# A fused LSH attention and FFN kernel: the probabilities of two head pairs of the first 256 tokens go through fp16 halves and DMA turns instead of fp32 turns on TensorE

## The chip, the cores and the metric

The kernel runs on one core of one Trainium2 chip. The metric is the device time of one execution in microseconds, the median of several runs; lower is better. The kernel before took 817.67 us (median of 3 runs, 816.54 to 818.07).

Five engines work in parallel, each through its own instructions in order: PE (TensorE, matrix products; its weight loads are listed as PEld), DVE (VectorE), ACT (ScalarE), POOL (GpSimd) and SP (SyncE, which here issues all DMA transfers). An instruction waits on semaphores for those of other engines on which it depends, and everything behind it on its engine waits too.

## The reference

```python
q_bits = (np.einsum('bhsd,dk->bhsk', q, proj) > 0)      # 6 hash bits per token, the same for k
mask = q_bucket[:, :, :, None] == k_bucket[:, :, None, :]
scores = np.where(mask, scale * (q @ k.T), -1e9)
attn = exp(scores - max); attn = attn / (attn.sum(-1) + 1e-9)
x = attn @ v                                            # 4 batches, 8 heads, 768 tokens, 64 dims
h = x.reshape(3072, 512) @ w_in                         # 512 -> 2048
g = h * np.tanh(softplus(h))                            # mish
out = g @ w_out                                         # 2048 -> 512
```

The inputs are 64-bit floats in memory and are converted on the chip. The products need more than fp16's precision. Most of the kernel gets it from two fp16 halves of each factor (a high half, and a low half that holds the rest) and three products: high by high, low by high, high by low. In the first units, fp32 products are used in some places, since those need no splitting ahead of them.

## The kernel before

**Units and slots.** The 3072 tokens are 12 units of 256 tokens (three per batch). A unit's attention is 8 slots: 4 pairs of heads by 2 blocks of 128 queries. Slot n of unit 0 has pair n // 2. One slot runs through this chain:

- S (`att_front`): PE multiplies the 128 queries with 768 keys of both heads into PSUM. The scores of slots 0 to 7 go alternately to `ps_s` and `ps_b`, later ones all to `ps_s`.
- Row maximum (DVE, L978), then scale and bias (`mb`, on DVE at L961 to L968 or on POOL at L972 and L973).
- Two exponentials (`att_exp`, ACT, L991), one per head, into a ring of three fp32 tiles `pb`, with the row sums.
- `att_back`: the sums' reciprocals (L1021), then the probabilities are turned (keys onto partitions) into `PT`, a ring of two pairs.
- V (`att_pv`): PE multiplies values with turned probabilities; the result goes to `X`, the unit's token block for the FFN.

**The two ways to turn.** In unit 0 (`if u == 0`), `pe_turn` turns the fp32 tile on PE: groups of three 128x128 turns (L434) into the PSUM tile `ps_l`, every fourth into `ps_t`, each group followed by a copy on ACT (L437) or DVE (L438). A group must wait until the bank's last copy is done. The probabilities are not yet divided by their sums: PE spreads the reciprocals over a tile (`rb`, L1072), ACT or DVE copies it (`rc`, L1075, L1076), V is an fp32 product (L1062) and DVE multiplies (L1079). In all other units the tile is first split into halves (`hl`): the high half is probability times reciprocal in fp16 (L390 on POOL, L392 on ACT, L393 on DVE), the low half the rest (L408 on DVE, one instruction; on POOL two, L414 and L415). One DMA turn per head and slot (L472) brings both halves to `PT`, and V is an fp16 product of three parts (L1088, two pairs at a time).

**Keys and queries.** In unit 0, pairs 0 and 1 have fp32 scores (L948): the keys are turned (L450) and their hash words come from a product with the sign weights `pw` (L461; `pw` is filled by DVE at L530). Pairs 2 and 3 have fp16 keys in two halves, turned by DMA, with hash bits (L739, L743, L748), and scores at L937.

**FFN.** For each unit 8 steps H (`ffn_h`, first product), mish on ACT, then O (`ffn_out`, second product). In unit 0 they are fp32 (L1120, L1169), later fp16 halves (L1130 to L1132, L1179 to L1181). H0, the first of all, needs all four pairs of unit 0 in `X`. The weights come in as 64-bit floats, are joined to fp32 (L594, L597, L601, L607), and are split later (`w_split`).

**What sets the order.** All operations are recorded with their alternatives (engine and cost), and `ORDER` is a table of numbers that gives the order in which they are issued, with a letter for the alternative (a, or none, is the first). The table fixes each engine's order and which engine does what; nothing is decided at run time. Semaphores are set from the dependences.

Of the kernel before, what the change touches and what calls it, by code (L numbers as in the profile page):

```python
# [23 lines left out]
PT = 12  # L24
# [69 lines left out]
137 7 9 8 50 20 0 5 11 19 12 22 1 2 3 4 76 80 29 81b 13 37 6 77b 14 15 10 25 33 26 30b 38 17 27 28 18 34 39 52  # L94
60 61 35 62 41 56 54 63 57 55 21 42 48 51 53 24 23 31 78 36 32 64 65 16 86 91 138 92 79 87 147 40 88 82 117 83
43 118 44 119b 93 89 66 109 110 111 153 90 94 120 67 112 154b 132 107d 46 108 133 113 95 115 68 114 116 124
125b 155 121 126 101 84 45 134 136 135 156 127b 178 96 128 140b 148 141 47 58 149 85 122d 123 97 99 142 139b
98b 143 129 168d 179 180d 100 174 176 69 175 177 170 130 157 171b 131 172 173b 204 205b 169 70 145b 182 189
144b 102 158 159 181 161b 190b 71 193 291 194 195 185 191 150 186 192 220 221 103 222d 183b 187 206 160b 196
188 197 104 223 212 152 146 49 151 162 59 105 106 213b 207 216 218 217b 219b 214 215b 184 353 224 243 163 239  # L100
164 244 245b 241 248 240 242 233c 270 368 307 210d 208 235 254 236 255 249 209b 237 246 238 247 225 256 271
250 257 234 272d 262 263 268 266 292 198 273 226 267b 211 227 293 165 294 269 251 283 284 349 350 264 303 265
285 295 166 304b 354 305 296 258 199 200 309d 286b 310 311c 260c 261 306 274 281 313 253 252 232 228 282 312b
322 201 317 364 287 365 288 289 290 366 318 319 355b 323 324 308 320 321 367 330b 331 315 338 339 72 231 203
202 167 229 397 369b 314 329 316 325 297 298b 275 276b 340 333 341 230 332b 334 342 73 370d 299 336 425c 277
74 426 371 399 378 379 380 335 328 302 400 398 300 373 424 423 351 337 301 280 381 427 372b 374 382 389c 411
376 259 375 278 279 406 429 458 428 390 412 452 407 352 391 383 384b 393 392c 395 326 327 385 453 408d 409 410
415d 343 344c 356c 416 451 430 456 345 431 432 394 377 459 386 418 346 457 396 401 417b 454 433 387 348 347
413 419 455 75 357 434 443d 488b 460 421 444 461 420 388 422 441 404 435 436 414 402 445 489 490b 447 437 462d
463 464 478d 403 446c 449 479 405 465 438 466b 471 472b 487 523 518 493 494 495c 486 358 359 467 496 480b 482b  # L110
497 448 481b 484 360 491 510 525 532 511 442 450 361 512b 533 534 535 362 526 524 468 483 513b 492 439 546 514
474 536 552 485 469 470 537 519b 475c 476 516 473 520 538c 539 553 515 517 586 540b 521 554 440 477 498 499b
500 501 555d 542 522 541c 556 557 573b 574 575 548 549b 550 527 503 502 544 577 590 545 543 578 528 530 504
505b 591 592 547 588 506 594 593 507 576b 595d 587 581 612 603 604 551 582 583b 579 596 598c 529 559 558 531
589 597 613 599 580 363 618 600 560 561 562 614d 616 584b 615 632c 563 564c 601 566 651 508 509 585 633 647
634c 648 655 659 640 617 567 649 636 650 652 664 653 605 635 656 565 619 620 621 660 654 638 622 623c 625 568
569 602 639 661d 609 668 606 641 663 662 681b 682 683c 642 626 637 570b 691 607b 608 685 657 665 666 571b 627
692 628 693d 572 624b 643b 782 672 644 645c 646 695 694 669 610b 658 723c 724 629 630b 684b 687 696 734 735
670b 673 783 697 675 725b 727 736d 738 686 726 631 698 737 688 690 689 732 786 731 749 674 667 699c 701 729
740d 741 791 742c 744 676 728 787 788 700 750 751 702 730 745 799 703 704 706 743b 677b 671 678 746 739 733  # L120
803 781 752 753 773b 800 784c 774 776 775 785 790 679b 804 705b 707 708 710 709 711 794 748 824 712 801c 779
777b 795 796c 802b 789 713 792 714c 716 780 747 778 825 839 680 798 797 816c 817 818b 715b 819 826 827 828 829
820 822 830 807 808 842 611 717 754 755 821 847 823 810 831b 832 833b 809 811 756 757 805 843 844 845 835 846
840 718 859 841 836 834c 719 721b 720b 758 759 860 722 760 837 838 769 861 871 872 863 873b 874 812 862b 864
875 876d 806 813 762 866 793 877 887 891 888 761 889b 892 865 879b 895 763 867 896 897d 898 848 878c 882 890b
880 868 884 904 764 765 885b 893c 899 883 881 849 850c 900 770 923 766b 852b 913b 914 771 767 922 908 924 768
925 905 901 915 916 926 917 927 928c 853 772 909 918 894 919 1026 920 929 930c 906 939 932b 910 902b 911 912
940 814b 869 968 854 921 972 941d 943 942 954 851c 903 931c 934 907 855 857 945 946 856 955 956c 947b 949b 969
973 1027 957 958 959c 937 936 982 970c 1028 933 935 960 961 948b 951b 858 971 963 976 815 944 977 978 979c 950
964 952 962 965b 938 986 967 953 981 980 995c 974c 1029 1067 1031 983 987 1005 1004 996 997c 999b 975b 988  # L130
998b 1001b 1006 1007b 1009 1008 966 1066 1010 1011 1012b 990 1158 1021 870 886 1032 1192 1193 984b 993 991 992
994 1022 1023 1019 1003 1033 1069 1030 1194 1024 1000 1014 1025 1039d 1050 1002 1015 1223 1068 985 1013c 1040
1016b 1017 1051 1052d 1041c 1070 1071c 1053 1043 1054 1195 1055c 1042b 1034 1044 1073 1018 1082 1077 1020 1038
# [20 lines left out]
1465c 1467 1408 1496 1512d 1383 1807 1516 1513 1514 1528d 1455 1456 1497 1529 1474 1385 1386 1519 1538 1520
1539 1540c 1499 1587 1517b 1530b 1532b 1541 1387 1468 1469 1483 1498 1542 1543c 1544 1545 1484 1470 1531b
1518b 1534 1591 1466c 1427c 1521 1522 1554 1641 1277 1500 1642 1523 1588 1547b 1555 1643 1556 1533 1535 1537
1536 1583 1508b 1557 1558 1509 1428 1584 1524 1569 1471b 1546b 1472b 1548 1473 1429c 1560b 1561 1570 1571c
# [1188 lines left out]
```

## Time and profile before

| | before |
|---|---|
| median of 3 runs | 817.67 us |
| the profiled execution's own time | 817.2 us |
| its span, first to last instruction | 815.4 us |
| granted TensorE clock | 1.0 |
| busy share PE, DVE, ACT, POOL | 98, 74, 77, 52% |
| starts on PE: S0, S4, S6, S8, S9, S10, H0 | 14.9, 37.0, 46.4, 56.0, 64.4, 71.6, 73.9 us |
| starts of V0, V1, V2, V3 | 40.7, 51.6, 61.7, 68.9 us |
| HBM read, written | 35.65, 6.29 MB |

The page gives each engine's busy time and its share of the span. A view by stage gives the same in chosen stretches; the timeline lists instructions of one engine in order of time, with the idle time ahead of each and what ended it; the groups put together instructions of one line and shape, with their mean duration; the waits add up who waited for whom. An engine's line shows how long an instruction takes, and the difference between two starts what it costs in a dense row, which on PE is less, since products overlap.

### The profile page before, as it was taken

Reading aid. Unit: us, or ns where it says so; the run is one execution under the profiler, and the core shown is the slowest. Engines: PE = TensorE matmul, PEld = TensorE weight load, DVE = VectorE, ACT = ScalarE, POOL = GpSimd, SP = SyncE. Lnnn points to the kernel's source line nnn. Section 1 sums busy time; section 2 is a strip of 40 time slices with the busy share of each in tenths; the row PEclk is TensorE's granted clock in tenths of the full one; section 3 lists DMA queues with packets and bytes.
Section 4 is the critical chain, followed back from the end, with each engine's and each line's share of the span. In section 5 each row is a group of like instructions: output and inputs, shape, how many; then the busy total and the mean of one; then the engine's idle time right before and its main releaser. Section 6 shows DMA issues by size and latency. Waiting matters only on the chain.

```text
span 815.4 us, 17000 instructions
## 1 busy us (share of the span) xinstructions
PE 798.2 (98%) x6546; PEld 549.6 (67%) x6546; DVE 602.9 (74%) x1103; ACT 624.9 (77%) x976; POOL 426.9 (52%) x434
## 2 busy tenths in 40 slices
PE   8899999999999999999999999999999999999998
PEld 5556666666676776676666676667676676776674
DVE  5888999988898778887887767768877675566211
ACT  4889998888696769889679698989779785677211
POOL 3564446554356773733585564344646758845120
PEclk9999999999999999999999999999999999999999
DMA  7958998989999969989989959999989577466200
GB/s 253 219 174 221 240 246 196 191 156 206 217 160 182 203 116 181 170 158 216 185 172 155 195 117 151 197 213 192 167 140 169 107 139 145 81 124 133 50 27 27
DMA packets 395489, 134.29 MB, mean 165 GB/s; under 512 B 365456, under 2 KB 386448, under 8 KB 395408
## 3 DMA queue, kind: packets, MB, share of 16 engines
q1 hardware_dynamic: 395408, 133.21, 81.2%
q8 instruction: 51, 0.84, 0.4%
q14 instruction: 30, 0.25, 0.1%
HBM read 35.65 MB, written 6.29 MB: 51 GB/s over the span
## 4 chain that ended last, share of the span: by engine, by line
PE 47%; ACT 1%; DVE 1%; DMA 1%; issue 0%; POOL 0%; SPq 0%; ACTq 0%; DVEq 0%
PE ps_s L937 7%; PE ps_o L1179 6%; PE ps_o L1181 6%; PE ps_o L1180 6%; PE ps_acc L1130 5%; PE ps_t L1088 5%; PE ps_acc L1132 5%; PE ps_acc L1131 5%; ACT pb L991 1%; DVE svb L978 1%; DMA out_dram<-ffb 1%; PE ps_t L739 0%; ACT L1315 0%; DVE hl L408 0%; ACT tok L480 0%
## 5 line engine op out<-in xcount | busy, mean ns | idle before, releaser
L991 ACT ACTIVATE pb<-ps_s,svb 128x768 f32<-128x768 f32 x184 | 180.9, 987 | 87.4 <-DVE svb L968 36.7
L978 DVE TENSOR_REDUCE svb<-ps_s 128x2 f32<-128x1536 f32 x92 | 161.3, 1753 | 40.2 <-PE ps_s L937 33.7
L1130 PE MATMUL ps_acc<-X,wo 128*128 128x256 f16 x616 | 167.9, 273 | 0.3 <-ACT ffb L1151 0.3
L1132 PE MATMUL ps_acc<-X,wo 128*128 128x256 f16 x616 | 167.9, 273 | 0.0
L1131 PE MATMUL ps_acc<-X,wo 128*128 128x256 f16 x616 | 167.9, 273 | 0.0
L1315 ACT ACT_TABLE_LOAD x117 | 150.1, 1283 | 2.0
L408 DVE SCALAR_TENSOR_TENSOR hl<-pb,svb,hl 128x768 f16<-128x768 f32 x131 | 140.3, 1078 | 13.8 <-POOL hl L390 9.8
L1181 PE MATMUL ps_o<-wi,ffb 128*128 128x512 f16 x352 | 133.4, 379 | 0.0
L1180 PE MATMUL ps_o<-wi,ffb 128*128 128x512 f16 x352 | 133.4, 379 | 0.0
L1179 PE MATMUL ps_o<-wi,ffb 128*128 128x512 f16 x352 | 133.4, 379 | 0.0
L937 PE MATMUL ps_s<-KT,QT 128*128 128x512 f16 (+1 forms) x656 | 120.1, 326 | 2.1 <-ACT pb L991 1.8
L390 POOL TENSOR_SCALAR hl<-pb,svb 128x768 f16<-128x768 f32 x68 | 71.0, 1046 | 75.9 <-DVE svb L1021 28.8
L937 PEld LDWEIGHTS <-QT 128*128 128x128 f16 x672 | 64.2, 98 | 40.5 <-issue 8.3
L1088 PE MATMUL ps_t<-PT,VT 128*64 128x256 f16 x1584 | 90.7, 273 | 0.0
L1088 PEld LDWEIGHTS <-VT 128*64 128x64 f16 x1584 | 84.8, 110 | 8.1 <-issue 7.6
L1151 ACT ACTIVATE ffb<-ps_acc,smalls 128x512 f32<-128x512 f32 x88 | 58.5, 684 | 33.5 <-PE ps_acc L1132 32.0
L415 POOL TENSOR_TENSOR hl<-pb,hl 128x768 f16<-128x768 f32 x45 | 75.0, 1667 | 3.8
L414 POOL TENSOR_SCALAR pb<-pb,svb 128x768 f32<-128x768 f32 x45 | 44.4, 987 | 48.0 <-ACT hl L392 21.4
L1131 PEld LDWEIGHTS <-wo 128*128 128x128 f16 x616 | 60.2, 98 | 13.3 <-issue 1.5
L1130 PEld LDWEIGHTS <-wo 128*128 128x128 f16 x616 | 60.2, 98 | 12.6 <-issue 0.5
L1132 PEld LDWEIGHTS <-wo 128*128 128x128 f16 x616 | 60.2, 98 | 7.0
L1181 PEld LDWEIGHTS <-ffb 128*128 128x128 f16 x352 | 34.4, 98 | 41.6
(240 smaller groups left out, 1300.5 us busy)
## 6 DMA issues: line engine op xcount, KB each, us to landing
out_dram<-ffb SPq DMA_DIRECT2D x22, 256.0 KB, 2.7
stg<-in_v_dram SPq DMA_DIRECT2D x13, 384.0 KB, 4.0
stg<-in_k_dram SPq DMA_DIRECT2D x12, 384.0 KB, 4.0
wo<-in_q_dram SPq DMA_DIRECT2D x9, 512.0 KB, 4.9
stg<-in_moe_w_in_dram SPq DMA_DIRECT2D x8, 512.0 KB, 4.6
stg<-in_moe_w_out_dram SPq DMA_DIRECT2D x6, 512.0 KB, 4.6
PT<-hl SPq DMA_TRANSPOSE x176, 4.1
wo<-in_moe_w_out_dram SPq DMA_DIRECT2D x5, 512.0 KB, 4.7
```

What stands on the lines that cost most here:

```text
L408: return [("DVE", 215 + 1.035 * n, port(lambda: nc.vector.scalar_tensor_tensor(out=dst, in0=src, scalar=sc, in1=hi, op0=ALU.mult, op1=ALU. ...
L937: nc.tensor.matmul(ps[:, hh * S + c0 * P:hh * S + c1 * P], QTb[:, u % 2, sl, qi], KTb[:, j, sl, hh * NCH + c0:hh * NCH + c1].rearrange("p ...
L978: op("max", [("DVE", 1755, lambda: nc.vector.tensor_reduce(out=sv[:, 0], in_=ps.rearrange("p (h e) -> p h e", e=S), axis=AX.X, op=ALU.max, ...
L991: EXP[n, hh] = op("exp", [("ACT", 1075, lambda hh=hh, t=t: nc.scalar.activation(pb[:, t], HOMES[n][0][:, hh * S:(hh + 1) * S], AF.Exp, bia ...
L1088: nc.tensor.matmul(pv[hh * D:(hh + 1) * D, y * 256:(y + 1) * 256], vt[:, w, hh * NCH + c], pt[:, hh, a * NCH + c].rearrange("p s t -> p (s ...
L1130: nc.tensor.matmul(o, wh, X[:, 0, c], start=(c == 0), stop=False)
L1131: nc.tensor.matmul(o, wh, X[:, 1, c], start=False, stop=False)
L1132: nc.tensor.matmul(o, wl, X[:, 0, c], start=False, stop=(c == NCC - 1))
L1179: nc.tensor.matmul(PS[f"o{s}"], gh, wh, start=first, stop=False)
L1180: nc.tensor.matmul(PS[f"o{s}"], gh, wl, start=False, stop=False)
L1181: nc.tensor.matmul(PS[f"o{s}"], gl, wh, start=False, stop=last)
L1315: for fn in plan.ordered("exp", lambda x: nc.scalar.preload_act_table_set(sets[x])):
```

## The change

In unit 0, pairs 2 and 3 (`j >= P32`, with `P32 = 2`) take the way of all further units: their probabilities are split into halves and turned by DMA, and V is a product of fp16 halves, one pair at a time. `X` of unit 0 stays fp32, so its result is scaled by a power of two (`iv`, one new DVE instruction) in one instruction on ACT or DVE. The halves of V of these two pairs, which were made behind the value product, are now made ahead of it.

```diff
+P32 = 2
 ...
+        iv, ivn = raws["iv"] = small([NPAIR], F32)
+        dve("iv", 165, lambda: pow2(iv, h[:, :, 1], 254 - SC - PT), [f"{hn}v"], [ivn])
 ...
-        if u == 0:
+        if u == 0 and j < P32:
             for hh in range(2):
                 t = (2 * n + hh) % NP_
                 pe_turn(pt32(pr, hh)[:, :, s], pb[:, t], [f"p{t}"], [pt_name(n, hh)])
 ...
+        if u == 0 and j >= P32:
+            def pe1():
+                pt, vt = PTb[:, p % 2], VTb[:, j]
+                steps = [(c, a, w) for c in range(NCH) for a, w in ((0, 0), (1, 0), (0, 1))]
+                for x, (c, a, w) in enumerate(steps):
+                    for hh in range(2):
+                        nc.tensor.matmul(pv[hh * D:(hh + 1) * D, 0:256], vt[:, w, hh * NCH + c],
+                                         pt[:, hh, a * NCH + c].rearrange("p s t -> p (s t)"),
+                                         start=(x == 0), stop=(x == len(steps) - 1))
+            op(f"V{p}", [("PE", 2080, pe1)], [(f"pt{p % 2}", 0, 4 * NKV), f"VT{j}.h", f"VT{j}.l"], [pvn], bb=True,
+               takes="sh")
+            iv, ivn = raws["iv"]
+            x32 = x_w[:, 0, j * 256:(j + 1) * 256]
+            op("x_f", [("ACT", 467, lambda: nc.scalar.activation(x32, pv[:, 0:256], AF.Copy, scale=iv[:, j:j + 1])),
+                       ("DVE", 410, lambda: nc.vector.tensor_scalar(out=x32, in0=pv[:, 0:256], scalar1=iv[:, j:j + 1],
+                                                                    scalar2=None, op0=ALU.mult))],
+               [pvn, ivn], [(xn, j, j + 1)], frees="sh")
+            return
 ...
+    for j in range(P32, NPAIR):
+        later(2 * P32 - .5, v_prep, 0, j)
 ...
-            if u == 0:
+            if u == 0 and j < P32:
                 v_prep(0, j)
 ...
 ORDER = """
-137 7 9 8 50 20 0 5 11 19 12 22 1 2 3 4 76 80 29 81b 13 37 6 77b 14 15 10 25 33 26 30b 38 17 27 28 18 34 39 52
```

The whole `ORDER` table is new, from its first number to its last, so the change also reorders everything else. Lines behind L166 move by a few (L978 becomes L980, L961 L963, L968 L970, L1021 L1023, L1079 L1099, and so on).

At the start of the program DVE did this before, up to the sign weights (`KT` copies are turned keys, the rows at L485, L501, L871, L875 are small scalars):

```order
L358 MEMSET ones 128x128
L358 MEMSET floors 128x1
L453 COPY KT<-ps_t 128x384
L358 MEMSET floors 128x4
L453 COPY KT<-ps_l 128x384
L501 TENSOR_SCALAR smalls<-ps_t 128x1
L485 TENSOR_SCALAR smalls<-smalls 128x1
L375 TENSOR_REDUCE smalls<-ffb 128x1
L377 TENSOR_SCALAR smalls<-smalls 128x1
L453 COPY KT<-ps_s 128x384
```

Behind these came L875, L485, L871 and then L530, which fills `pw`. Now the same engine starts so:

```order
L358 MEMSET floors 128x1
L358 MEMSET floors 128x4
L375 TENSOR_REDUCE smalls<-ffb 128x1
L377 TENSOR_SCALAR smalls<-smalls 128x1
L358 MEMSET ones 128x128
L453 COPY KT<-ps_s 128x384
L530 TENSOR_SCALAR pw<-pj_79 64x6 x4
```

`pw` moved ahead of two of the key copies and of the query's scale; `ones`, which PE's warm-up reads, moved behind the threshold (L375 reads the identity that POOL makes).

Between the maxima of S7 and S8, DVE had weight joins (L607), copies of turned probabilities (L438) and a result product (L1079):

```order
L978 TENSOR_REDUCE svb<-ps_b 128x2
L607 SCALAR_TENSOR_TENSOR wi<-wo,wi 128x1024
L1079 TENSOR_TENSOR X<-ps_t,ffb 128x256
L1021 RECIPROCAL svb<-svb 128x2
L438 COPY PT<-ps_l 128x3x128
L1021 RECIPROCAL svb<-svb 128x2
L607 SCALAR_TENSOR_TENSOR wo<-stg,wo 128x1024
L978 TENSOR_REDUCE svb<-ps_s 128x2
```

Between the same two maxima it now has a high half (L393) and two low halves (L408), with the scale and bias of S7 (L963, L970) and the sums' reciprocal:

```order
L980 TENSOR_REDUCE svb<-ps_b 128x2
L963 TENSOR_SCALAR svb<-svb,smalls 128x2
L970 TENSOR_TENSOR svb<-svb 128x2
L408 SCALAR_TENSOR_TENSOR hl<-pb,svb,hl 128x768
L1023 RECIPROCAL svb<-svb 128x2
L393 TENSOR_SCALAR hl<-pb,svb 128x768
L908 TENSOR_SCALAR smalls<-smalls 128x2
L408 SCALAR_TENSOR_TENSOR hl<-pb,svb,hl 128x768
L980 TENSOR_REDUCE svb<-ps_s 128x2
```

The joins moved behind S8's maximum, the copies are gone, the halves are new.

On SP, which issues the DMA transfers, these rows led up to the first turn of probabilities into `PT` before:

```order
L468 DMA stg<-in_moe_w_out_dram 128x1024 x2
L468 DMA wo<-in_moe_w_out_dram 128x1024 x2
L468 DMA stg<-in_moe_w_in_dram 128x2x512 x2
L468 DMA wi<-in_moe_w_out_dram 128x1024 x2
L472 DMA_TRANSPOSE QT<-tok_65 128x8x128
L472 DMA_TRANSPOSE PT<-hl 128x12x128
```

Around the first turns into `PT` it has this now:

```order
L468 DMA stg<-in_moe_w_out_dram 128x1024
L468 DMA X<-in_q_dram 128x8x128
L472 DMA_TRANSPOSE PT<-hl 128x12x128 x7
L468 DMA stg<-in_moe_w_in_dram 128x2x512
L472 DMA_TRANSPOSE PT<-hl 128x12x128
L468 DMA wi<-in_moe_w_out_dram 128x1024 x2
```

The eight new turns stand ahead of weight loads that came ahead of every `PT` turn before, and a load of queries moved next to the first turn.

More of the change, by code (lines that the diff above doesn't have):

```diff
@@ L99 @@
[L99 to L133, printed above, removed]
@@ L154 @@
[L154 to L157, printed above, removed]
-1773 1562b 1525 1564 1549b 1585b 1572 1550 1551 1597 1552 1589 1526 1563 1573 1574d 1598 1565 1485 1553 1592
@@ new lines @@
+937 938 946 947 896b 940 959 960 847 924 939 941 948 949 950c 952 953 1182 1016 804 965 966 933 942 956 975
+967 968 963 951 970 969 984c 1017 1018 994 964b 954 976 985 987 972 995 996d 997 986b 988 973b 998 999d 1057
+1020 1000 955 992 979 989 980 982 1001 1010 981 983 1011 1012 990b 1013 1003 1014 1028c 875 991 1021 1002b
+977b 1005 1029 1004 1006 1058 993 1039 1007 1062 1022 1008 1059 1040 1041 1042 974b 1030b 1032 1043 1023 1031c
+1019 1063 1183 1044 1034 1045 1046b 1048b 1066 1067 1068c 1069 1070 1184 1242 1033 1047b 1025b 1024 1050 978
@@ new lines @@
+1168b 1170 1179 1180 1146 1135 1169c 1172 1196 1137 1109 1161 1190 1241 1038 1171 1173 1155b 1162 1164 1197
+1207 1198 1208 1188c 1213 1163 1124 1138 1174 1175 1159b 1200 1214 1165 1201 1209d 1191 1205 1215 1217 1211
+1210 1225b 1192 1156 1199 1236 1194 1237 1226 1227 1228 1238 1218 1193b 1202b 1239 1203 1267 1204 1271 1219
+1231b 1229 1240 1256c 1257 1258b 1260 1275 1276 1277 1230 1272 1284 1268 1273b 1269b 1394 1259c 1262 1278 1279
+1280 1195 1261 1232 1216c 1243 1244 1297 1270 1220 1298 1274 1299b 1307 1308 1263 1206 1245 1246 1247c 1249
@@ new lines @@
+1422 1343 1430 1431 1432 1433 1424 1434 1411 1385 1255 1414 1412 1266 1321 1296b 1358 1359 1435c 1436 1413
+1415 1446 1423b 1426b 1393b 1425 1427 1352 1322 1491 1319 1437 1360 1361 1447 1323 1405 1448d 1362 1428 1429
+1373 1439 1363 1324b 1364c 1449 1438 1441 1450 1325b 1464 1465 1396 1466 1440 1366 1397 1326 1442 1367 1475
+1492 1476 1493c 1477 1406 1467c 1494 1495 1504 1478 1468b 1479 1480d 1481 1482 1499 1470 1365b 1452 1496 1368
+1443 1469 1484b 1369 1370 1371b 1500 1501 1502 1418b 1503 1483 1444 1374 1445 1463 1508 1527 1453 1409c 1375
@@ new lines @@
+1454c 1580 1471 1376 1485 1372 1486b 1456 1517 1518 1410 1416 1630 1457 1519c 1528 1529c 1509 1505 1455 1530
+1521 1531 1472 1488 1510c 1532 1533 1520 1497b 1506b 1576 1458 1459 1543 1487 1512 1522 1534c 1419b 1489b 1460
+1473b 1544 1545c 1525 1572 1526 1474 1536b 1417b 1511b 1535b 1538b 1461 1547 1523 1524 1546 1498 1631 1513
+1515 1549c 1540 1558 1670 1507 1577 1573 1550 1514 1516 1632 1551 1633b 1559 1542 1541 1557 1586 1553 1560
+1462 1537 1552c 1539 1555 1554 1556 1562 1561 1574b 1563 1564 1565c 1566 1567b 1575b 1581 1582 1583 1584 1585
@@ new lines @@
+1967 2000 2045 1977 1978 1939b 1999 2066 2044 2026 2046 1979b 2047d 2024b 2048 1941 2049 2020c 2021b 2050d
+1881 1981 1982 1850 2027 2029 1980b 2041 2028 2051 2030 2059 2061 2062 2063 2040 2042 2052b 2067 2064 2110
+1983 2078 2054 1984 2055 2065 2079c 2053c 2025 2068 1988 2080 2081 2056b 2057 2090 2091 2092 2069b 2093 2082b
+2083 2094 2084 2103 1989 2043 2106 2071 1990 2085 2114 2107 2095d 2072 2086 2096 2111 2098 2058 2060 2119 1991
+2097c 2011 2115 2116c 2099b 2100 2117 2118 2104 2101b 2102 2073 2123 1986 2132d 2133 1985 2134c 2033c 2120
@@ new lines @@
+2309 2306 2310 2312 2340 2319 2256 2321 2341 2342 2303b 2333b 2322 2373 2323 2311 2343 2344 2346c 2307b 2355
+2332b 2313 2304 2335 2356 2347 2348c 2374 2338 2337 2369 2357d 2358 2350 2377 2359 2370 2308 2334 2336 2349b
+2360d 2352 2361 2362 2364b 2351 2353 2378 2345 2379 2380 2363 2366 2365 2339 2387 2383 2371b 2382 2381 2406
+2396b 2372 2397 2398 2400b 2407 2408b 2410 2409 2411d 2412 2367 2413b 2354 2375c 2388 2376 2399b 2391 2394
+2368 2389c 2392 2401 2404 2422 2405 2384 2385 2386b 2393 2395 2423 2424 2402 2425 2414 2417b 2403 2415 2426
@@ new lines @@
+2520 2518 2438 2535 2546c 2542c 2539 2557 2558 2525 2477 2526 2547 2527c 2528 2529 2530b 2533b 2543 2478 2480
+2531 2532 2534 2559 2560 2548 2549 2550 2551b 2561 2562 2552 2563 2566 2555 2553 2564 2554 2556 2569 2570 2571
+2573 2574 2577 2572 2581 2578 2593 2585 2582 2597 2583c 2565 2454 2567b 2586 2568 2575 2576b 2587 2588 2594
+2595b 2601 2596 2579c 2580 2598 2590 2589 2599c 2584b 2602 2603 2592 2591 2610 2609 2600b 2604 2612 2605 2614
+2611 2606 2607c 2608 2620 2621b 2623 2624 2622 2613 2615 2618b 2616b 2619 2617
```

155 lines of the change are left out of this document (80 added, 75 removed).

## The prediction

> **What bounds the kernel now.** First the head of the page, then the busy time of each engine by stage (columns: stretch, its length, busy us and instructions of PE, PE's weight loads, DVE, ACT, POOL, then granted clock, DMA share, GB/s).
>
> ```profile
> span 815.4 us, 17000 instructions
> PE 798.2 (98%) x6546; PEld 549.6 (67%) x6546; DVE 602.9 (74%) x1103; ACT 624.9 (77%) x976; POOL 426.9 (52%) x434
> ```
> ```profile
> 0.00:14.90 14.90, 11.84 (x111) 9.02 (x112) 6.71 (x24) 6.78 (x13) 4.62 (x11) 1.00 0.76 265
> 14.90:38.50 23.60, 20.60 (x173) 13.26 (x172) 19.65 (x45) 18.05 (x38) 11.96 (x18) 1.00 0.94 225
> 38.50:68.90 30.40, 27.99 (x233) 18.00 (x231) 25.51 (x47) 26.16 (x55) 18.49 (x19) 1.00 0.61 185
> 68.90:73.80 4.90, 4.82 (x40) 2.90 (x41) 3.86 (x8) 4.90 (x9) 1.90 (x2) 1.00 1.09 225
> 73.80:160.00 86.20, 85.57 (x516) 58.37 (x515) 80.50 (x122) 78.19 (x118) 42.18 (x38) 1.00 0.98 220
> 160.00:240.00 80.00, 77.48 (x700) 54.38 (x700) 71.54 (x130) 66.70 (x101) 39.02 (x43) 1.00 0.98 185
> 240.00:800.00 560.00, 558.32 (x4727) 387.53 (x4722) 393.81 (x728) 422.27 (x645) 306.86 (x303) 1.00 0.79 150
> ```
>
> From 73.8 us on PE is all but full: 0.6 us idle up to 160, 2.5 up to 240, 1.7 up to 800. Before that it idles 3.1 + 3.0 + 2.4 = 8.5 us, and there DVE and ACT are as full as PE. 73.8 is no accident; it is where the first FFN product H0 starts, right behind S10 (the scores of slot 10):
>
> ```profile
> 71.61 2.25 PE L948 MATMUL ps_s<-KT,QT 64*128 64x256 f32 x15
> 73.85 3.70 PE L1120 MATMUL ps_acc<-X,wi 128*128 128x256 f32 x16
> ```
>
> So the program has two parts. Behind H0, time is PE's work. Ahead of H0 it is a chain through four engines (scores, row maximum on DVE, exponential on ACT, turn, value product). Everything that the change takes from PE lies ahead of H0; it counts only as far as it brings H0 forward.
>
> **What PE loses.** Starts on PE's timeline give the dense price of each removed thing:
>
> ```profile
> 25.50 0.55 PE L434 MATMUL ps_l<-ffb,pb 128*128 128x128 f32 x3
> 25.88 0.49 PE L434 MATMUL ps_t<-ffb,pb 128*128 128x128 f32 x3
> ...
> 61.69 2.81 PE L1062 MATMUL ps_t<-PT,hl 128*64 128x256 f32 x24
> 64.44 2.25 PE L948 MATMUL ps_s<-KT,QT 64*128 64x256 f32 x15
> 66.61 0.66 PE L1072 MATMUL ps_t<-ffb,svb 128*64 128x128 f32 x8
> 67.20 0.55 PE L434 MATMUL ps_l<-ffb,pb 128*128 128x128 f32 x3
> ```
> ```profile
> 101.01 4.12 PE L1088 MATMUL ps_t<-PT,VT 128*64 128x256 f16 x72
> 105.14 1.46 PE L937 MATMUL ps_s<-KT,QT 128*128 128x512 f16 x8
> ```
>
> Three turns step 0.38 us; four slots have 16 such groups: 6.1 us. An fp32 value product steps 2.75 us; the fp16 one costs 4.13 us for two pairs, so 2 x 2.75 - 4.13 = 1.4 us go. The spread of the reciprocals steps 0.59, twice: 1.2 us. Together **8.7 us** of PE work, 1.1% of the span. That is the ceiling, and I don't think it is reached.
>
> **What DVE and ACT get.** The groups of the front (14.9 to 73.9 us; busy us, mean ns of one, idle before), and one of DVE's waits between 38.5 and 68.9 (us in total, times, longest):
>
> ```profile
> L991 ACT ACTIVATE pb<-ps_s,svb 128x768 f32<-128x768 f32 x12 | 11.9, 996 | 2.5 <-DVE svb L968 2.4
> ...
> L437 ACT COPY PT<-ps_l 128x384 f32<-128x384 f32 x14 | 6.6, 475 | 2.2 <-PE ps_l L434 2.1
> ```
> ```profile
> L438 DVE COPY PT<-ps_l 128x384 f32<-128x384 f32 x10 | 5.5, 554 | 3.4 <-PE ps_l L434 3.4
> L408 DVE SCALAR_TENSOR_TENSOR hl<-pb,svb,hl 128x768 f16<-128x768 f32 x2 | 2.1, 1027 | 0.0
> L607 DVE SCALAR_TENSOR_TENSOR wi<-wi 128x1024 int32<-128x1024 int32 x1 | 1.2, 1214 | 0.0
> L1076 DVE TENSOR_SCALAR ffb<-ps_t 128x256 f32<-128x256 f32 x2 | 0.8, 425 | 0.7 <-PE ps_t L1072 0.6
> L393 DVE TENSOR_SCALAR hl<-pb,svb 128x768 f16<-128x768 f32 x1 | 0.6, 620 | 0.1
> ```
> ```profile
> DVE PT L438 <- PE ps_l L434: 2.1, 4, 1.2
> ```
>
> The stretch that matters runs from the row maximum of S4 to the scale and bias of S9, since S10, and with it H0, stands behind those:
>
> ```profile
> 38.53 1.76 DVE L978 TENSOR_REDUCE svb<-ps_s 128x2 f32<-128x1536 f32 x1
> ...
> 66.72 1.76 DVE L978 TENSOR_REDUCE svb<-ps_s 128x2 f32<-128x1536 f32 x1 [0.65 <-PE ps_s L948]
> 68.51 0.23 DVE L961 TENSOR_SCALAR svb<-svb,smalls 128x2 f32<-128x2 f32 x1
> 68.78 0.16 DVE L968 TENSOR_TENSOR svb<-svb 128x2 f32<-128x2 f32 x1
> ```
>
> It lasts 30.4 us and DVE is busy 25.5 of it. By the two orders, between the same two points DVE loses 5 copies out of PSUM (six become one, 5 x 0.55 = 2.8), one scaled copy of the spread (0.4), one result product (same size, 0.4; now two on ACT) and two weight joins that now stand later (2.4). It gains seven more low halves (one becomes eight, 7 x 1.03 = 7.2), two high halves (1.2) and a low half of V (the same operation and size, 1.0). 25.5 - 6.0 + 9.4 = **28.9 us**. With DVE never idle the stretch shortens by 1.5 us; with the old 4.9 us of idle it grows to 33.8, by 3.4. Of the 4.9 idle, 2.7 were waits for the turns (2.1) and a spread (0.6) that go; what is left, 2.2, would give 31.1. I take 1.2 left, nearer to never idle, because the chain between two slots loses its round trips through PSUM: 30.1, **0.3 us shorter**. ACT gives up some twelve copies at 0.475 (5.7 us) and takes four high halves and two weight steps, at least 4 x 0.62 + 2 x 1.21 = 4.9 us by DVE's prices; it comes out about even, and its 4.2 us of idle in that stretch cover what an ACT instruction costs above DVE's. On POOL, which has 11.9 of the 30.4 us free, the other halves and V's preparation hide; without that cover each costs at least its DVE price, 1.03 us for a low half.
>
> **The head start.** Score slot 0 starts at 14.89 and the program's new order moves what it waits for:
>
> ```profile
> 1.03 3.60 PE L364 MATMUL ps_l<-ones 128*128 128x128 bf16 x32 [1.03 <-DVE floors L358]
> ...
> 6.53 0.82 PE L450 MATMUL ps_s<-ffb,wi 128*64 128x128 f32 x12
> ...
> 14.89 2.25 PE L948 MATMUL ps_s<-KT,QT 64*128 64x256 f32 x15
> ```
> ```profile
> 9.07 1.59 DVE L530 TENSOR_SCALAR pw<-pj 64x6 f32<-64x6 f32 x4
> ```
>
> The sign weights pw, on which all three hash products ahead of S0 depend, stood at 9.07; now they follow the copy of the first turn of K. The warm-up starts about 1 us later than at 1.03 (its ones stand behind the threshold, which waits for POOL's identity) and so ends near 5.6; a turn of K takes 0.82, its copy less than that, and I put pw at about 7.2 and S0 1.5 us earlier (an estimate from these rows). Between S0 and S4 the old turns of pairs 0 and 1 go on, so I let **1.3 us** of it arrive at S4. Bounds: 0, and the 1.9 by which pw itself comes earlier.
>
> **The last turn.** The low half of pair 3 that finishes last is followed on DVE by a high half, S9's maximum, another low half and the scale and bias: 0.62 + 1.76 + 1.03 + 0.4 = 3.8 us; the two exponentials (L991, 0.996 each) add 2.0 before S10 can start: 5.8. The value product V3, ahead of S10 on PE, needs the turn and its own 2.07:
>
> ```profile
> PT<-hl SPq DMA_TRANSPOSE x176, 4.1
> ```
>
> 4.1 + 2.07 + 0.1 = 6.3, so S10 is held **0.4 us**. DMA was at a share of 0.61 in the stretch and SP had time, so the eight turns themselves cost nothing; if SP's turn is late by x, H0 is late by x.
>
> **Behind H0.** PE's work there is the same instructions. By the new order DVE takes over halves from POOL all through the program, and at 80.5 of 86.2 us it is close to full until 160. I add 0.2 us of PE idle, bounded by -1 and +3 (PE's idle there was 0.6 + 2.5).
>
> **PE ahead of the scores.** Between 38.5 and 68.9 PE itself stood before turns whose bank a copy still held, and the scores of the next slot stood behind them:
>
> ```profile
> PE ps_l L434 <- ACT stg L480: 0.8, 1, 0.8
> ```
>
> This was the longest; PE's whole idle of 2.4 us there is the upper bound, 0 the lower, and I take **1.0 us** off.
>
> **Sum**: -1.3 - 0.3 + 0.4 + 0.2 - 1.0 = -2.0. The profiled execution took 817.2 us (its span and 1.8 us around it), so 815.2; the runs shown have a median of 817.67, 0.5 above it, and a result is read against that median. 0.2% of it, 1.6 us, is about what a measurement can tell.
>
> **Rivals.**
> - *PE's whole 8.7 us arrive.* Then DVE must finish the stretch more than 6 us sooner, with 28.9 us of work in 30.4: that speaks against. For it: half the joins and halves could slide behind H0. Time 808.5, up to 812.5 for half of it.
> - *DVE takes it all back.* Stretch at 31.1 to 32 us and a head start that dies before S4: 816 to 819, no difference.
> - *Slower: DVE's low halves hold POOL's scale and bias.* Two rows of POOL, and what DVE did at the second:
>
> ```profile
> 34.09 0.31 POOL L972 TENSOR_SCALAR svb<-svb,smalls 128x2 f32<-128x2 f32 x1 [1.86 <-DVE svb L978]
> ...
> 42.54 1.19 POOL L972 TENSOR_SCALAR svb<-svb,smalls 128x2 f32<-128x2 f32 x1 [3.02 <-DVE svb L978]
> ```
> ```profile
> 42.34 1.22 DVE L607 SCALAR_TENSOR_TENSOR wi<-stg,wi 128x1024 int32<-128x1024 int32 x1
> ```
>
> The same tiny operation took 0.31 us alone and 1.19 us beside a two-input DVE operation: 0.9 us. Now two of the slots S5 to S9 take scale and bias from POOL, and pay this; in the new order it is three (S5, S6, S8), two POOL operations each, with low halves on DVE right around them. At most that is 3 x 2 x 0.9 = 5.4, less the 1.8 paid now: 3.6. Half of it, with DVE keeping its old idle: 33.8 + 1.8 - 30.4 = 5.2, less the head start of 1.3 and with the turn's 0.4: 4.3, so 821.5. It decides from a stretch of 33.4 us on (30.4, the 2.1 up to 819.3, and 0.9 net head start). The Trainium skill, page "SBUF — State Buffer", section "SBUF: two separate sides", states the rule: the port pair shared by VectorE and GpSimd is an exclusive lock held for a whole instruction, taken also by a VectorE operation with two SBUF inputs against a GpSimd one that reads SBUF. The two rows above agree; by this rule a POOL operation can wait out a whole low half, and the sum would be this rival's.
> - *The change doesn't do what it says.* The orders show the 16 groups, two spreads and fp32 products gone, so no chance of its own.
>
> **Chances.** Forecast (813 to 816.6) 0.42, PE's gain arrives in larger part (808.5 to 813) 0.16, no difference (816 to 819) 0.22, slower by the lock or by late turns (819.3 to 823) 0.20. From the forecast's own range 0.06 falls inside 0.2%: faster 0.52, same 0.28, slower 0.20. The range that leaves out no more than 0.2 is 810 to 820.5.
>
> **What would show it.** H0's start in the new trace carries the whole sum: at 72 the forecast, under 68 the first rival, at 74 the second, from 76 the slower one. S0's start near 13.4 shows the head start, S4's row maximum near 37.2 what is left of it; DVE's busy time between S4's maximum and S9's bias near 29 us the middle term; the wait of V3 for DMA the turn. I am wrong if PE's idle behind H0 differs from 4.8 us by more than 3, since then the planner's new order and not this change sets the time.

## The result and the profile after

The changed kernel takes **826.39 us** (median of 4 runs, 824.62 to 827.47) and the kernel before, beside it, 817.25 (816.54 to 818.07): a ratio of 1.011, with a 95% interval of 1.0092 to 1.0128. It is slower by about 9 us. The profiled execution took 827.39 us, 10.2 us more in its span than that of before (825.6 against 815.4).

The head of its page, then the view by stage in stretches that fit the new stages (columns as in the prediction):

```profile
span 825.6 us, 16893 instructions
PE 796.3 (96%) x6506; PEld 547.6 (66%) x6506; DVE 619.3 (75%) x1089; ACT 618.7 (75%) x969; POOL 406.9 (49%) x421
```
```profile
0.00:12.00 12.00, 9.58 (x96) 7.17 (x96) 4.35 (x21) 4.64 (x10) 4.88 (x11) 1.00 0.86 278
12.00:36.50 24.50, 21.14 (x172) 13.48 (x171) 17.99 (x40) 17.64 (x38) 17.48 (x24) 0.93 0.91 216
36.50:65.50 29.00, 22.34 (x155) 13.46 (x155) 28.18 (x49) 25.85 (x48) 18.16 (x19) 0.84 0.95 225
65.50:74.50 9.00, 8.09 (x96) 5.95 (x94) 7.70 (x12) 8.31 (x15) 3.14 (x4) 0.94 1.16 244
74.50:160.00 85.50, 82.86 (x486) 56.12 (x485) 77.75 (x111) 77.15 (x117) 39.66 (x32) 0.98 0.94 225
160.00:240.00 80.00, 76.16 (x658) 52.87 (x656) 72.44 (x134) 66.73 (x103) 28.03 (x38) 1.00 1.03 192
240.00:800.00 560.00, 554.29 (x4736) 386.51 (x4734) 405.67 (x719) 415.81 (x640) 292.68 (x294) 1.00 0.82 152
```

PE has less work but more idle time, and its clock is no longer 1.0 everywhere. Behind H0 it idles 2.6 + 3.8 + 5.7 = 12.2 us, where it was 4.8. On PE's timeline of the changed kernel the scores of slots 0, 2, 3, 9 and 10, H0, and slot 16:

```profile
11.99 2.25 PE L950 MATMUL ps_s<-KT,QT 64*128 64x256 f32 x15
...
22.43 3.70 PE L950 MATMUL ps_s<-KT,QT 64*128 64x256 f32 x15
...
30.32 2.25 PE L950 MATMUL ps_b<-KT,QT 64*128 64x256 f32 x15
...
63.18 3.80 PE L950 MATMUL ps_s<-KT,QT 64*128 64x256 f32 x15
...
72.29 2.25 PE L950 MATMUL ps_s<-KT,QT 64*128 64x256 f32 x15
74.53 7.15 PE L1140 MATMUL ps_acc<-X,wi 128*128 128x256 f32 x32
...
126.07 2.25 PE L950 MATMUL ps_s<-KT,QT 64*128 64x256 f32 x15
```

H0 starts at 74.53, 0.7 us later than before (73.85). Slot 16 started at 120.50 before, so 4.9 of the 10.2 us are added between H0 and slot 16, and the remaining 4.6 behind it. Not all of the 4.9 is lost time, since the new order does more work there: four products of the first O step more (1.7 us) and eight small ones less (0.2). Behind slot 16 PE idles 13.7 us instead of 8.3. What happens ahead of slot 15 in the changed kernel, on PE, ACT, POOL and DVE:

```profile
113.89 1.88 PE L1189 MATMUL ps_o<-wo,ffb 128*128 128x512 f32 x4
117.86 2.72 PE L939 MATMUL ps_s<-KT,QT 128*128 128x512 f16 x8 [2.09 <-ACT pb L993]
```
```profile
115.75 0.99 ACT L993 ACTIVATE pb<-ps_s,svb 128x768 f32<-128x768 f32 x1 [2.48 <-POOL svb L975]
```
```profile
110.85 3.71 POOL L974 TENSOR_SCALAR svb<-svb,smalls 128x2 f32<-128x2 f32 x1 [1.01 <-DVE svb L980]
114.65 1.07 POOL L975 TENSOR_TENSOR svb<-svb 128x2 f32<-128x2 f32 x1
```
```profile
108.99 1.75 DVE L980 TENSOR_REDUCE svb<-ps_s 128x2 f32<-128x1536 f32 x1
110.66 1.01 DVE L408 SCALAR_TENSOR_TENSOR hl<-pb,svb,hl 128x768 f16<-128x768 f32 x1
111.59 1.28 DVE L408 SCALAR_TENSOR_TENSOR wo<-wi,smalls,wo 128x1024 f16<-128x1024 f32 x1
112.78 1.22 DVE L607 SCALAR_TENSOR_TENSOR wo<-wi,wo 128x1024 int32<-128x1024 int32 x1
113.92 0.61 DVE L393 TENSOR_SCALAR hl<-pb,svb 128x768 f16<-128x768 f32 x1
```

Read from the bottom up: slot 14's maximum is ready at 110.7. Its scale on POOL, two numbers per partition, starts at 110.85 and ends at 114.56. Beside it DVE ran three instructions with two inputs in a row, to 114.00, and then a high half with one input, to 114.53. The exponentials start at 115.75, and PE stands 2.09 us for them. Behind the stall the next products run at a lower clock (0.86 in the stretch from 112 to 124 us, 1.00 there in the kernel before): slot 15's scores take 2.72 us instead of 1.46.

Behind 148 us PE's waits (us in total, times, longest) are many and small. The first is the changed kernel's, the second that of before:

```profile
PE ps_s L939 <- ACT pb L993: 7.8, 13, 1.3
```
```profile
PE ps_s L937 <- ACT pb L991: 1.7, 4, 0.6
```

### The profile page after: what moved, and what is told of

Read it like the earlier page. It is cut to its first block, busy times and chain, and to the rows that moved or that the text cites. A ratio compares the mean times of both kernels' runs of the same rounds, so it can differ in the third digit from the quotient of the medians.

```text
span 825.6 us, 16893 instructions
## 1 busy us (share of the span) xinstructions
PE 796.3 (96%) x6506; PEld 547.6 (66%) x6506; DVE 619.3 (75%) x1089; ACT 618.7 (75%) x969; POOL 406.9 (49%) x421
## 5 line engine op out<-in xcount | busy, mean ns | idle before, releaser
L980 DVE TENSOR_REDUCE svb<-ps_s 128x2 f32<-128x1536 f32 x92 | 161.3, 1753 | 41.5 <-PE ps_s L939 34.5
L408 DVE SCALAR_TENSOR_TENSOR hl<-pb,svb,hl 128x768 f16<-128x768 f32 x134 | 145.6, 1092 | 13.6 <-POOL hl L390 11.6
L390 POOL TENSOR_SCALAR hl<-pb,svb 128x768 f16<-128x768 f32 x52 | 51.4, 989 | 82.6 <-DVE svb L1023 34.9
L415 POOL TENSOR_TENSOR hl<-pb,hl 128x768 f16<-128x768 f32 x50 | 83.8, 1676 | 4.2
L414 POOL TENSOR_SCALAR pb<-pb,svb 128x768 f32<-128x768 f32 x50 | 49.8, 996 | 69.0 <-ACT hl L392 32.9
L392 ACT ACTIVATE hl<-pb,svb 128x768 f16<-128x768 f32 x68 | 62.3, 929 | 25.2 <-DVE svb L1023 6.7
L1151 PEld LDWEIGHTS <-wo 128*128 128x128 f16 x616 | 60.2, 98 | 13.7 <-issue 1.0
```

The costliest lines, as they stand in the source:

```text
L408: return [("DVE", 215 + 1.035 * n, port(lambda: nc.vector.scalar_tensor_tensor(out=dst, in0=src, scalar=sc, in1=hi, op0=ALU.mult, op1=ALU. ...
L980: op("max", [("DVE", 1755, lambda: nc.vector.tensor_reduce(out=sv[:, 0], in_=ps.rearrange("p (h e) -> p h e", e=S), axis=AX.X, op=ALU.max, ...
L1151: nc.tensor.matmul(o, wh, X[:, 1, c], start=False, stop=False)
```

## The experiments

In `ORDER` each number is one operation, in its order of issue. "The order of before" means the same operations in the sequence that the old table gave them, and on the engines that it chose. Each ratio is against runs of the kernel before on the same chip (medians of 816.99 to 817.67 us).

**Joined orders.** Is the time behind H0 lost by the change, or by the newly planned order of the rest? The first three kernels cross the two tables, at H0 or at slot 24.

The changed program, in the order of before from H0 on:

```diff
 ... 166b 327 326b 350b 331 232
-386 388 332 233 333 274 275b 294 334 335 ...
+254 253 315 316 317 332 168 386 322 309 318 294 295b 274 ...
```

> The changed program with its own order up to H0, and from H0 on the rest of the work in the order of the kernel before. Theory 1 (the newly planned order of the rest costs the time behind H0): PE idles near 5 us behind H0 again, H0 stays at 74.5, and the time is 817 to 819. Theory 2 (the loss behind H0 follows from the state in which the front leaves the other engines): PE idles 10 us or more behind H0 and the time stays at 825 to 827.

The program of before, in the new order from H0 on:

```diff
 ... 72 231 203 202 167 229
-397 369b 314 329 316 325 297 298b ...
+369b 259b 314 332c 532 334 333b 357b 397 399 230 340 275 ...
```

> The kernel before with its own order up to H0, and from H0 on the rest in the order of the changed kernel; no pair of unit 0 is computed differently. Theory 1 (order of the rest): 824 to 827, with 11 to 13 us of PE idle behind H0 and the wait ahead of slot 15. Theory 2 (state of the front): 816 to 819, with 4 to 6 us.

The changed program, in the order of before from slot 24's scores on:

```diff
 ... 700 668b 814 696
-783 784 785 701 813 829 ...
+631 783 813 701 790c 768 784 ...
```

> The changed program in its own order up to the scores of slot 24 (206 us), the remaining work in the order of the kernel before. If the loss behind H0 is made in the first units behind the front, where PE waits for ACT and the clock drops, the time is 824 to 826; if it is spread over the whole new order, 820 to 822.

Measured: 829.81 us (ratio 1.0151, interval 1.0136 to 1.0166), 825.67 (1.0108, 1.0089 to 1.0126) and 825.41 (1.0101, 1.0074 to 1.0127). The second says that the new order costs 8 us without any of the change, though its joint has a part in this: PE's first wait, 1.40 us, stands ahead of slot 11. And the first contradicts it: with the old order behind H0 the changed program is no faster. It jams once, at the joint. The PE timeline and the ACT timeline of that kernel:

```profile
83.96 0.16 PE L489 MATMUL ps_t<-smalls,ones 128*128 128x1 bf16 x1 [5.97 <-DVE hwo L494]
```
```profile
79.27 1.13 ACT L587 ACTIVATE wo<-wo 128x1024 f32<-128x1024 f32 x1 [6.01 <-DMA wo<-in_moe_w_out_dram]
```

The old order joins a weight chunk there (315 to 317). Its two loads are issued at 72.0 and 72.9 us in this kernel, those into the same tile at 54.5 and 58.9 in the kernel before; ACT waits 6.0 us for them, and all that follows on ACT and DVE stands behind it. From slot 11 to the end this kernel takes 736.7 us, before 734.3: the jam is nearly all. The third kernel is 6.7 us late at slot 24, of 9.5 in its whole span: most of the loss is made ahead of that slot.

**Mending the joint.** The late chunk is prepared behind slot 11's exponentials, and the new order runs up to slot 11:

```diff
 ... 309 328 74 367
-329 296 359d 360 75 279 168 330 ...
+253 168 359d 329 296 414c 75 415 360 368 ...
```

> As the changed front with the order of before behind it, but the joint is mended: the changed program's own order runs to slot 11's scores, and the weight chunk whose load arrived 7 us late at the old joint (and its successors in the same buffers) is prepared after slot 11's exponentials. Theory 1 (the newly planned order of the rest is the cost): no jam at the joint, slot 16 at most 3 us later than in the kernel before, time 818 to 821. Theory 2 (the front hands over a debt of weight work that has to be paid somewhere before slot 24): the jam only moves, slot 24 is 6 us or more late, time 824 or more.

831.25 us (1.0165, 1.0138 to 1.0192): the jam only moved, to slots 13 and 14. Two more kernels of this kind:

```diff
 ... 407 423 422 374
-410 444 432 433 477c ...
+400 401 375 376 402 444 432d ...
```

> The changed program in its own order up to just ahead of the scores of slot 14 (about 106 us, where slot 13 is 1.7 us later than in the kernel before), the remaining work in the order of the kernel before; at that place only four instructions that the order of before counts on are not done yet. Theory 1: the 2 to 3 us of wait and the low clock ahead of slot 15 are gone, PE idles under 5 us behind slot 14, and the time is 819 to 822. Theory 2: slot 15 still comes 4 us late and the time stays at 824 or more.

828.69 us (1.0141, 1.0126 to 1.0156): again a wait, 5.59 us ahead of slot 15, where ACT works through weight steps of both orders before the exponentials. And the change put into the places of the old operations (the edit in words):

```diff
-tp, tcp (16 groups of turns and copies of pairs 2 and 3), rb, rc, fp32 V2, V3
+hi, lo, ptturn in the places of the first groups; halves of V2 ahead of slot 6, of V3 ahead of V3
```

> The changed computation in the order of the kernel before: only the turns, copies and spreads of pairs 2 and 3 are replaced in their places by high halves (4 on ACT, 3 on POOL, 1 on DVE), low halves (8 on DVE) and turns by DMA, the preparation of V2 and V3 is moved ahead, and both result products stand on ACT; everything else, all of the work behind H0 included, stays where it stood. DVE has 30.8 us of work between slot 4's maximum and slot 9's bias by the prediction's prices, so H0 at 74 to 76. Theory 1 (the newly planned order costs the time behind H0): PE idles 3 to 6 us behind H0 and the time is 817 to 820. Theory 2 (the change's work on DVE leaves a state that the rest pays for): 10 us or more of idle behind H0 and 823 or more.

837.26 us (1.0242, 1.0225 to 1.0259). Here the front itself falls apart (slot 10 at 86.4 instead of 71.6), so it says little of the rest. Each of these kernels ran nearly as densely as before once its jam was over, which is no proof for the order: a jam also gives the other engines time to catch up. So the joint's own price had to be measured.

**The late chunk alone,** in the kernel before, with nothing computed differently:

```diff
 ... 232 228 282 312b
-322 ... 323 324 ... 329 ... 325 ... 328
 ... 427 372b 374 382
+322 323
 389c 376
+324 329 325 328
 ...
```

> The kernel before, nothing computed differently, with one weight chunk (its two unpackings, join, square and two loads, and the first steps of its successor in the same buffers) prepared behind slot 11's exponentials instead of ahead of H0, as in the kernel with the mended joint. If weight chunks that are handed over late are what costs the time in the joined kernels, the same jam appears ahead of slots 13 and 14 and the time is 823 to 828. If not, 817 to 819.

824.41 us (1.0088, 1.0073 to 1.0104). PE's waits of this kernel between 74 and 250 us:

```profile
PE ps_s L929 <- ACT pb L983: 6.7, 7, 4.2
```

One weight chunk, joined on DVE at 90.0 us instead of 69.0 (with the first steps of its successor in the same buffers), costs 7 us with no change at all. The jams of the joined kernels are of that kind, and they neither convict nor clear the front. In the changed kernel the same join stands later still, at 95.16, but its own order is made for that: from 74 to 112 us PE idles 0.2 us of 38 there.

```profile
74.00:112.00 38.00, 37.78 (x221) 26.45 (x218) 36.84 (x53) 35.44 (x52) 16.61 (x14) 1.00 1.05 264
```

**A joint without missing work.** At slot 19's scores all weight chunks are joined, and nothing that the other order counts on is missing:

```diff
 ... 559 558 531 589
-597 613 599 580 363 618 ...
+508 655 597 509 613 647 ...
```

> The kernel before, nothing computed differently, in its own order up to the scores of slot 19 (147 us), from there the order of the changed kernel; at that place nothing that the new order counts on is missing, and all weight chunks are joined. In the changed kernel PE idles 9.5 us from 160 to 800 us, in the kernel before 4.2. If these waits belong to the new order alone, they come here too: 820.5 to 823. If they follow from what the changed front and the stall at slot 15 left over, 817 to 818.5.

824.50 us (1.0088, 1.0074 to 1.0102), more than expected even by the first theory. This kernel has nothing of the change and is level with the kernel before up to slot 19 (0.2 us ahead); PE then idles 10.5 us from 148 to 800 us where it idled 4.3. Its waits behind 148 us:

```profile
PE ps_s L929 <- ACT pb L983: 6.4, 10, 1.4
```

So the new order makes such waits by itself, with no change ahead of it. That it alone makes those of the changed kernel doesn't follow; the last kernel of the next group bears on that.

**The port.** Slot 14's scale and bias move from POOL to DVE, behind the maximum (450):

```diff
-409 450 375 376 436 478 ... 402 411 438 451d
+409 450 451 375 376 436 478 ... 402 411 438
```

> The changed kernel with one operation pair moved: slot 14's scale and bias from POOL, where the first took 3.71 us beside four two-input operations of DVE, to DVE right behind slot 14's maximum. If the lock of the port that DVE and POOL share makes the stall ahead of slot 15 (2.09 us, and 2 us more by the clock that falls to 0.73 behind it), slot 15 starts at 115.5 to 116, slot 16 at 123 to 123.7 instead of 126.1, and the time is 822.5 to 824.5. If the stall follows from work that the front left over, ACT's exponentials come late all the same, slot 16 stays at 125.5 to 126.5, and the time at 825.5 to 827.

824.29 us (1.0094, 1.0079 to 1.0109). On DVE and PE of this kernel:

```profile
111.30 0.23 DVE L956 TENSOR_SCALAR svb<-svb,smalls 128x2 f32<-128x2 f32 x1
111.56 0.16 DVE L963 TENSOR_TENSOR svb<-svb 128x2 f32<-128x2 f32 x1
```
```profile
116.19 1.46 PE L932 MATMUL ps_s<-KT,QT 128*128 128x512 f16 x8
...
122.93 2.25 PE L943 MATMUL ps_s<-KT,QT 64*128 64x256 f32 x15
```

The stall and the low clock are gone, and slot 16 starts at 122.93 instead of 126.07 although slot 10 was 0.8 us later in this execution: 4.0 us between the two slots. The median falls by 2.1 only, and the intervals of the two ratios overlap. The changed kernel's runs lie in two groups, 827.4 (twice) and 824.6 to 825.4, and that the stall occurs only in the first would fit, but no trace of a run of the second was taken. Other traces bear on it. From slot 10 to slot 16 the three kernels with this pair on DVE (this one and the next two) take 49.8 to 49.9 us. With the pair on POOL and the same order in that stretch, the changed kernel, the one joined at slot 24 and the one with slot 8's pair on DVE (below) take 53.0 to 53.8 us, each with a scale of 3.71 us, in executions of 826.7 to 827.7 us. The one with small products of ones (below) takes 49.6 us, in an execution of 824.7 us, and its scale, beside the same row of DVE instructions, is this:

```profile
111.52 0.99 POOL L970 TENSOR_SCALAR svb<-svb,smalls 128x2 f32<-128x2 f32 x1 [1.57 <-DVE svb L976]
```

So the pair on POOL makes the stall, but not in every execution. All 23 pairs behind H0 on DVE:

> The changed kernel with all 23 scale and bias pairs that POOL does behind H0 moved to DVE, each right behind its maximum (0.4 us of DVE work each). If waits on POOL for the shared port are most of the time lost behind H0, PE's idle there falls from 12.2 to under 7 us and the time to 819 to 822. If only slot 14's matters, the time is that of the kernel above, or up to 2 us worse by DVE's added work.

824.73 us (1.0100, 1.0083 to 1.0117): the others cost nothing that shows. Both repairs together, the pair on DVE and the order of before from slot 19 on:

```diff
 ... 586 587 498 602
-636 549 550 588 603b ...
+588 569 356 607 589 549 ...
```

> The changed kernel with slot 14's scale and bias on DVE, in its own order up to slot 19's scores (150 us, 3.1 us later than in the kernel before) and from there in the order of before; nothing that this order counts on is missing there. If the waits behind 160 us belong to the new order alone, the shift stays at 3 us and the time is 820 to 822.5. If they follow from what the first 150 us left over, 823.5 to 825.

823.99 us (1.0085, 1.0068 to 1.0101). Its own expectation puts 823.5 to 825 down to what the first 150 us left over, and the time is not clearly below the 824.29 with the new order. This kernel was 2.4 us late at slot 19, 4.2 at slot 22 (the joint), stays at that to slot 66, and gains 2.6 more in small waits between slots 67 and 81. These last waits come in each kernel that has the changed front and the old order behind it, not in the one with the late chunk alone; their cause stays open. So the new order can't be called the only cause of the waits behind slot 16.

**What holds H0.** Three kernels edit the front. The result product of pair 1 (258) ahead of slot 8's maximum and two joins (230, 205) behind slot 9's scale and bias, with the joint of the first kernel:

```diff
-290 228 272 ... 347 258 284 ... 230 205 ... 311 306 312
+258 290 228 272 ... 347 284 ... 311 306 312 230 205
```

> As the first kernel of this call, and in the front the result product of pair 1 stands ahead of the row maximum of slot 8 on DVE, and two weight joins (1.22 us each) with their squares and loads stand behind the scale and bias of slot 9. If the front is short of DVE work only (a full DVE between the maximum of slot 4 and slot 9's bias), 2.4 to 2.9 us leave that stretch and H0 starts at 71.6 to 72.2 with the time 2 to 3 us under the first kernel's. If the stall of 3.65 us ahead of the token turn and the clock that drops behind it set H0, the scores of slot 9 come 3 us or more earlier and H0 at 71 or earlier. If neither (the exponentials or the last turn hold slot 10), H0 stays within 0.5 us of 74.5.

Small products of ones where PE idles behind slot 8:

```diff
+            if n == SLOTS:
+                for _ in range(28):
+                    nc.tensor.matmul(ps_l[:, 0:P], ones, ones, start=True, stop=True)
```

> The changed kernel with 28 small matmuls of ones into a free bank behind slot 8's scores, where PE idles 3.65 us and its granted clock falls to 0.5. If the low clock is on the chain to H0, the token turn takes 1.1 instead of 1.98 us, slot 9's scores 2.25 instead of 3.80, and H0 starts at 73.0 instead of 74.5. If DVE's full load sets H0, H0 stays at 74.2 to 74.5.

Slot 8's scale and bias (291) to DVE, and a low half (306) behind slot 9's (312):

```diff
-290 228 272 ... 284 291d 292 ... 311 306 312
+290 291 228 272 ... 284 292 ... 311 312 306
```

> The changed kernel with two edits of DVE's order: slot 8's scale and bias move from POOL (1.04 us for the first of the two operations) to DVE right behind the maximum, and the low half that stands between slot 9's maximum and its scale and bias goes behind them. The amount of work of DVE hardly changes (0.4 us more). If H0 is set by the chain maximum, scale, exponentials, scores through the one bank of slots 8 to 10, H0 comes 1.5 to 2 us earlier (72.5 to 73); if it is set by DVE's full load, it stays at 74.5 or comes later.

H0 came at 74.7, 75.5 and 75.15 us, never earlier; the times were 832.65 (1.0189, 1.0172 to 1.0206), 825.15 (1.0101, 1.0069 to 1.0133) and 825.98 (1.0100, 1.0071 to 1.0129). In the first, PE took the token turn 3.4 us earlier, and slot 9 then waited for its bank; in the third, slot 8's second and slot 9's first exponential waited for a low half:

```profile
57.74 1.09 PE L443 MATMUL ps_t<-ffb,X 128*64 128x128 f32 x16 [1.52 <-DVE X L1092]
63.22 4.02 PE L943 MATMUL ps_s<-KT,QT 64*128 64x256 f32 x15 [4.38 <-ACT pb L986]
```
```profile
62.46 0.99 ACT L986 ACTIVATE pb<-ps_s,svb 128x768 f32<-128x768 f32 x1 [0.43 <-DVE hl L401]
...
70.80 0.99 ACT L986 ACTIVATE pb<-ps_s,svb 128x768 f32<-128x768 f32 x1 [0.66 <-DVE hl L401]
```

The ring of three `pb` tiles closes the circle: an exponential may only overwrite a tile whose low half DVE has taken. So a low half can't be put off, and moving one wait shows the next. The products of ones and the two edits of DVE's order (291 and 306), with the mended joint:

> The three edits together: the mended joint with before's order behind it, the matmuls of ones behind slot 8, and the two edits of DVE's order. If each is right, H0 starts at 71 to 71.8 and the time is 3 us under that of the mended joint alone, 815 to 818; if DVE's load sets H0, it is that of the mended joint.

828.59 us (1.0141, 1.0116 to 1.0166), 2.7 under the mended joint, within overlapping intervals and with H0 at 76.2: a gain, if it is one, is not by this reason. No version beat the kernel before.

## Why the prediction was wrong

Forecast 815.2 us in a range of 810 to 820.5; it took 826.39. The profiled execution missed the sum by 12.2 us: 2.9 ahead of H0, which was to start at 71.65 (73.85 less 2.2) and started at 74.53, and 9.3 behind it. By the prediction's steps:

- **PE's loss of 8.7 us** came, but the clock took about half of it back. Ahead of H0 PE is busy 61.15 us against 65.25, 4.1 less: the scores of slots 2 and 9 took 3.70 and 3.80 us instead of 2.25, those of slot 7 2.70 instead of 1.46, at a granted clock of 0.93 and 0.84 in the two stretches from 12 to 65.5 us. The prediction had no term for the clock.
- **Head start, 1.3 us at S4: wrong.** S0 came 2.9 us earlier, at 11.99 (1.5 was expected), but S3 at 30.32, 1.9 us later than before (28.43), and S4's maximum at 39.77, not 37.2. The old turns between S0 and S4 didn't "go on" as they were: the new order set them among other work, and slot 2's scores alone lost 1.45 us by the clock.
- **DVE's stretch: right, in part by luck.** From S4's maximum to S9's bias it lasts 30.28 us (forecast 30.1) with DVE busy 29.14 (28.9), from this row of the view by stage:

```profile
39.77:70.05 30.28, 23.67 (x180) 14.62 (x180) 29.14 (x50) 26.55 (x48) 17.48 (x18) 0.83 0.96 209
```

Beside operations of POOL one low half took 1.93 us instead of 1.02 and one high half 1.27 instead of 0.62. The forecast had no such 1.6 us, so its other parts were too large by about as much.

- **PE ahead of the scores, -1.0: not there.** In the stretch of 36.5 to 65.5 PE idles 6.7 us, where it idled 2.4. The waits for `ps_l` are gone, but those for the bank `ps_t`, which DVE reads late, are longer than they were:

```profile
PE ps_t L450 <- DVE X L1099: 3.7, 1, 3.7
PE ps_t L1092 <- DVE hsum L745: 1.7, 1, 1.7
```

The last turn (0.4) was near: slot 9's exponentials end at 72.1, V3 at 72.4, and S10 starts at 72.29.

- **Behind H0, +0.2 with a bound of +3: this is the step that failed.** It said "PE's work there is the same instructions". They are, but their order is new, and PE idles 12.2 us there instead of 4.8, which is the case that the prediction named as its refutation. Of the 10.2 us between the two spans, 0.7 stand ahead of H0; 4.0 are the stall ahead of slot 15 and the clock behind it, which go when one pair of operations is moved off POOL; 0.9 more lie between slots 10 and 16, where the new order also does more work; 4.6 lie behind slot 16, where PE idles 5.3 us more, in small waits for exponentials. The kernel before makes such waits, and loses 7 us, when it takes the new order from slot 19 on. But the changed front with the old order from slot 19 on is no clear gain, so how much of the 4.6 us is the order's own stays open.
- **The slower rival had the right mechanism at the wrong place and price.** It put DVE's two-input operations against POOL's scale and bias ahead of H0, at 0.9 us each. There the three pairs (slots 5, 6, 8) cost 1.7 us over their price alone. Behind H0 one operation paid 3.4 us (3.71 against 0.31) beside three two-input operations in a row; beside the same row it took 0.99 in another execution, so the price is not fixed. By the Trainium skill's page "SBUF — State Buffer", section "SBUF: two separate sides", the shared port is held for a whole instruction and the other side blocks; the trace agrees that POOL blocks, but here it was let in only after the third instruction, not after the one that ran when it came.

Not settled: which of the new order's choices makes the waits behind slot 16, and what part of the first 4.9 us another order behind this front could save; the joints at H0, slot 11 and slot 14 brought late weight work with them. That one late chunk alone costs 7 us was shown; that the changed kernel itself loses time by this was not.

## What to carry to other kernels

Where a change comes with a newly planned order, price the order apart from the change: put the new order on the old computation, joined at a place where no work is missing, and look at the waits. In the kernel before PE idled 0.6% behind H0, and a late weight chunk cost 7 us, a late operation on two numbers 4: a program that full has little cover. Small operations on the path of the scores are safer off POOL while DVE runs a row of two-input instructions. Of the 23 pairs on POOL only one was seen to cost time, so look for it in the trace. To put an instruction with one input between the long ones was not tried.

## What the runs showed of the hardware

- A POOL operation on 128x2 numbers took 0.31 us alone, 0.99 to 1.19 when it was held by one two-input DVE operation and 3.71, in three traces, when it was let in only behind three in a row. In the execution with the products of ones, with the same order, the same operation came 0.7 us later and took 0.99. What decides between the two isn't shown.
- PE's granted clock fell behind short gaps. In the changed kernel no wait between 17 and 22.4 us is over 0.57, and still the next scores took 3.70 us instead of 2.25, at a granted clock of 0.55. Filling a gap didn't hold it: 28 products of ones took 1.74 us where 3.65 had been idle, gaps of 1.81 and 1.17 were left, and slot 9's scores took 4.02, at a clock of 0.50:

```profile
56.94 1.74 PE L953 MATMUL ps_l<-ones 128*128 128x128 bf16 x28
60.49 1.09 PE L443 MATMUL ps_t<-ffb,X 128*64 128x128 f32 x16 [1.81 <-DVE X L1095]
62.76 4.02 PE L943 MATMUL ps_s<-KT,QT 64*128 64x256 f32 x15 [1.17 <-ACT pb L989]
```

- The length of a gap didn't decide it. Behind 2.09 us of wait slot 15's scores took 2.72 us in the changed kernel, and 1.46, the full speed, in the kernel joined at slot 24:

```profile
117.98 1.46 PE L931 MATMUL ps_s<-KT,QT 128*128 128x512 f16 x8 [2.09 <-ACT pb L985]
```
